# 51 zero products on TensorE instead of 64, in a kernel that chains a gated recurrence and a cosine-gated feed-forward layer

## The chip, the cores and the metric

The kernel runs on one core of a Trainium2 chip. The metric is the device time of one execution in microseconds (us), as the median of several executions. A core has a TensorE (PE) that multiplies matrices into PSUM, a VectorE (DVE), a ScalarE (ACT) and a GpSimd engine (POOL), each with its own queue of instructions that it works off in order, and a SyncE (SP) whose queue issues nearly all DMA transfers here. PSUM is used as eight banks of 128 x 512 float32. Engines wait for each other through semaphores.

## The reference

Inputs are q, k, v and f_logit of shape (4, 8, 768, 48) (batch, heads, sequence, head width), and two weight matrices w_in (384 x 2048) and w_out (2048 x 384).

```python
f = 1 / (1 + exp(-f_logit))
for t in range(768):
    state = f[:, :, t, :, None] * state + einsum('bhd,bhe->bhde', k[:, :, t], v[:, :, t])
    y[:, :, t] = einsum('bhd,bhde->bhe', q[:, :, t], state)
x = y.transpose(0, 2, 1, 3).reshape(3072, 384)
h = x @ w_in
out = (h * cos(h)) @ w_out
```

## The kernel before, in words

The sequence is cut into pieces of 256 tokens, three for each of the four batches: 12 pieces, called pairs (a pair holds two blocks of 128 tokens, g = 0 and g = 1). The recurrence inside a pair is done with matrix products. The feed-forward part works in 13 units, the first two of 128 tokens, the rest of 256.

The steps of a pair n, with the line of the instruction in the profile:

- `f`, `k`, `q`, `v`: loads (L298). `ex`, `ln`, `fx`, `fy` (L331 to L349): the gate and its logarithm on ACT. `ad` (L365): sums of two tokens' logarithms on POOL, into a tile `sp`.
- `cum` (L376, L382, PE): running sums of the logarithms into one bank. `eb` and `ei` (L397; L393 for the first two pairs, ACT): exponentials of these sums, tiles `b` and `bi`. They are the readers of that bank.
- `qa`, `ka`, `qm`, `km` (L340 to L353, L406): q and k times the gates, mostly on POOL, into the tile `qk`, in two halves .0 and .1. `vb`, `vt` (L199): v rounded to bfloat16 and rearranged. Each of these copies is placed on ACT or POOL.
- `tq`, `tk` (L437, PE): transposes of the two parts of a `qk` half into a bank; `qkt` (L199): the copy out of it, on DVE or ACT. Pairs 6 to 11 transpose by DMA instead.
- `sc` (L458, PE): scores into two banks; `am` (L463, DVE): the masked copy out of them.
- `ps` (L481, PE): what the pair adds to the state; `st` (L499) and `sz` (L505), both on DVE: the state carried on and decayed.
- `y` and `yi` (L533, PE): the output inside the blocks and from the state before, two banks; `xe` (L199, ACT or DVE): the copy out to `x`.

The steps of a unit m: `h` (L581, PE) multiplies x by a part of w_in into two banks, `co` (L586, ACT) takes the cosine, `g` (L563, DVE) multiplies both; `o` (L597, PE) multiplies by w_out, `ot` copies out and `out` stores. The weights arrive in float32 in buffers of the pool for `g` (`w0.i` for w_in, `w1.i` for w_out, L284) and are rounded by `wc0.i`, `wc1.i` (L199, POOL or ACT).

The order of the work is written out by hand in `ORDER`, a list of words such as `sc1.0:T2`: the step, the engine's letter (T for PE, V for DVE, S for ACT, G for POOL, Y for SP), and the buffers or PSUM banks that its results take. Each engine gets its steps in the order of this list, and semaphore waits follow from what the steps read and write. A step that writes a bank waits for the readers of what stood there before. Steps on different banks of one PSUM tile are declared independent by `apart`, which looks back over the last 12 users of the tile.

The zero products are the steps `zf0` to `zf63` (L266). Each is one product of a 128 x 128 and a 128 x 512 tile of zeros, started afresh and written into one PSUM bank that nothing reads. They stand among PE's steps from its first instruction up to `h1.01`. A zero product, too, waits until the bank that it writes has been read.

The part of PE's order around the change, from 16 to 34 us of the profile, is (numbers after T are banks; a step without one goes on in the bank that an earlier step of the same value opened): `tk1.1`, eight zero products (T0), `cum3:T0`, three zero products (T0), `tk1.0`, `yi0:T6`, `y0:T7`, three zero products (T2), `sc1.0:T2`, seven zero products (T4), `sc1.1:T0`, `cum2:T4`, `ps1.0:T6,7`, `ps1.1`, three zero products (T2), `h0.00:T2`, `h1.00:T4`, two zero products (T0), `h1.01`, `yi1:T6,0`, `y1`, `h0.01`, `h2.11:T0` and so on. The readers of `cum3`'s bank stand in ACT's order as `vb1`, `eb3`, `ei3`, `vt1.1`, `xe0.0`, `ei2`, `eb2`; DVE's order there is `qkt1.1`, `qkt1.0`, `sz0.11`, `xe0.1`, `am1.0`, `sz0.10`, `am1.1`, a clearing of a state tile, `st1.00`, `st1.01`, `sz1.01`, `sz1.00`, `st1.11`, `st1.10`, `xe1.0`.

Of the kernel before, what the change touches and what calls it, by code (L numbers as in the profile page):

```python
# [54 lines left out]
st1.01:V km2.1:G co1.0:S0 sz1.01:V0 sz1.00:V st1.11:V yi1:T6,0 y1:T h0.01:T st1.10:V xe1.0:V1  # L55
sz1.10:V0 sz1.11:V xe1.1:S co0.0:S1 h2.11:T0 h2.10:T g0.0:V2 g1.0:V1 co2.1:S2 g2.1:V3 w1.1:Y0
h2.01:T6 f4:Y2 w1.3:Y4 h2.00:T co2.0:S1 h2.20:T2 h2.21:T h1.10:T4 co2.2:S0 h1.11:T g2.0:V h2.31:T0
h2.30:T co1.1:S2 co2.3:S1 g2.2:V g1.1:V wc1.3:G tk3.1:T6 tq3.0:T7 tq3.1:T qkt3.1:S2 h0.11:T2 tk3.0:T
h0.10:T o3.2:T6 sc3.1:T4 v2:Y0 qkt3.0:S3 co0.1:S2 am3.1:V0 g0.1:V g2.3:V o3.0:T o2.0:T7 o1.2:T4
o2.2:T o1.0:T sc3.0:T2 o0.2:T5 tq2.0:T0 tq2.1:T1 o0.0:T tk2.0:T wc1.1:S ex4:S ln4:S1 v3:Y1 ad4:G2  # L60
fy4:S vb2:S1 tk2.1:T vt2.0:S1 fx4:S vt2.2:S vt2.1:S vb3:G0 vt3.0:S0 am3.0:V1 qkt2.0:V0 qkt2.1:V1
o2.1:T o3.1:T f5:Y0 ex5:S sc2.1:T0 am2.1:V2 sc2.0:T2 o0.1:T am2.0:V3 o1.3:T o2.3:T o3.3:T ot2:V0
ot3:V1 ps2.1:T2 ps2.0:T vt3.2:G st2.00:V st2.01:V sz2.01:V1 q4:Y1 cum4:T3 o0.3:T o1.1:T sz2.00:V
ot1:V2 ps3.1:T6,7 vt2.3:G ps3.0:T sz3.00:V2 sz3.01:V ln5:S1 y2:T2,0 yi2:T xe2.1:V0 vt3.3:G vt3.1:G
y3:T4,6 yi3:T xe3.0:V1 ad5:G2 xe2.0:S ei4:S0 fx5:S eb4:S0 h3.20:T0 cum5:T4 eb5:S1 ei5:S1 v5:Y2 v4:Y0
st3.11:V xe3.1:V ot0:V3 k4:Y0 h3.21:T co3.2:S1 sz3.11:V0 st3.10:V sz3.10:V qa4:G h4.10:T2 h3.11:T4
h3.10:T h4.11:T h3.01:T6 h3.00:T co3.1:S2 g3.2:V1 g3.1:V qm4.0:G1 qm4.1:G vb4:G0 vb5:G1 co4.1:S0
ka4:G co3.0:S1 k5:Y1 q5:Y0 km4.1:G ka5:G h4.20:T0 h4.21:T h3.31:T4 h3.30:T g4.1:V2 fy5:S co4.2:S2
co3.3:S0 g3.0:V g4.2:V km5.0:G2 km4.0:G qa5:G vt4.2:G0 vt4.3:G qm5.0:G h4.30:T2 f6:Y1 f7:Y2 h4.31:T
tk4.1:T6 tq4.1:T o5.2:T7 o4.2:T0 tq4.0:T1 co4.3:S1 vt4.0:S ex6:S v6:Y2 out1:Y q6:Y1 out3:Y k6:Y0  # L70
out0:Y q7:Y2 out2:Y v7:Y0 qm5.1:G km5.1:G vt4.1:G k7:Y1 qkt4.1:V2 g3.3:V g4.3:V tk4.0:T tk5.0:T6
o5.0:T o5.1:T qkt4.0:V3 ps4.0:T4,5 ps4.1:T sc4.1:T2 st4.01:V st4.00:V sz4.01:V2 ex7:S vt5.2:S1
ln7:S1 ln6:S0 sz4.00:V st4.11:V am4.1:V0 tq5.0:T o6.2:T1 st4.10:V o5.3:T ot5:S2 o6.3:T tq5.1:T4
tk5.1:T o4.3:T sc4.0:T2 ad7:G2 sz4.11:V1 sz4.10:V qkt5.0:S0 fy7:S fx6:S cum7:T6 vt5.0:G ad6:G0
o4.1:T o4.0:T vt5.1:G vt5.3:G ka6:G eb7:S0 ei7:S1 fy6:S cum6:T5 ot4:S3 eb6:S2 ei6:S0 km6.0:G1
km6.1:G sc5.0:T6 qkt5.1:V1 am4.0:V1 y4:T0,2 yi4:T sc5.1:T4 ps5.0:T3 ps5.1:T am5.0:V2 fx7:S xe4.0:S0
vb6:S0 xe4.1:S o6.1:T h4.01:T6 h4.00:T co4.0:S1 ps6.1:T2,0 ps6.0:T st5.00:V sz5.00:V0 am5.1:V0
st5.01:V sz5.01:V sz6.01:V2 sz6.00:V h5.00:T4 h5.01:T zvt.2:G g4.0:V h5.21:T2 h5.20:T qa6:G qm6.0:G
vt6.1:G2 zsz.3:G ka7:G co5.0:S0 vb7:S1 yi5:T6,7 y5:T o6.0:T vt7.3:G0 co5.2:S1 xe5.0:S1 ot6:S0
g5.0:V1 h5.30:T4 h5.31:T co5.3:S0 zsp.1:G vt7.2:G vt6.3:G qm6.1:G km7.1:G2 vt7.0:G vt6.0:G km7.0:G  # L80
qa7:G st6.11:V st6.10:V xe5.1:V h6.20:T6 f9:Y0 k9:Y2 f8:Y1 tq6.0:Y2 out5:Y tq6.1:Y0 sz6.10:V0
sz6.11:V h6.21:T g5.2:V co6.2:S1 vt6.2:S h5.10:T0 h5.11:T co5.1:S2 g5.3:V g6.2:V3 h6.10:T2 h6.11:T
co6.1:S1 ex9:S ln9:S0 ex8:S g5.1:V qm7.1:G qm7.0:G ad9:G1 v8:Y0 f10:Y2 tq7.1:Y1 out6:Y tq7.0:Y3
g6.1:V o9.2:T4 o8.2:T5 o9.0:T o9.3:T q8:Y2 v9:Y2 q9:Y1 ps7.0:T0,1 sc6.1:T2 ps7.1:T sc6.0:T6 st7.01:V
st7.00:V am6.1:V0 am6.0:V2 ln8:S1 vb8:G0 ad8:G0 zqk.0:G o8.1:T o8.0:T o9.1:T o7.0:T2 cum9:T3 o8.3:T
sz7.01:V1 sz7.00:V yi6:T0 st7.10:V y6:T6 cum8:T7 o7.2:T o7.1:T o7.3:T fx8:S st7.11:V sz7.10:V2
ot8:V0 ot9:V2 xe6.0:V0 ot7:V1 sz7.11:V ex10:S ln10:S1 xe6.1:S fx9:S eb8:S2 ei9:S1 h7.30:T4 ei8:S0
fx10:S v10:Y0 k8:Y1 eb9:S1 sc7.1:T6 sc7.0:T2 ad10:G1 ka9:G h7.31:T h6.30:T0 h6.31:T am7.1:V0
am7.0:V2 co7.3:S1 fy9:S fy8:S fy10:S co6.3:S2 km9.1:G2 vt8.3:G2 vt7.1:G qa8:G qa9:G yi7:T6,7 y7:T
qm8.0:G0 q10:Y0 h6.00:T2 h6.01:T co6.0:S0 vb9:S1 qm8.1:G ka8:G km8.1:G km9.0:G km8.0:G vt9.1:G0  # L90
g7.3:V2 qm9.1:G vt9.3:G qa10:G qm9.0:G xe7.0:V2 xe7.1:V g6.3:V h7.00:T4 h8.11:T6 h7.01:T co7.0:S2
vt8.1:S h7.10:T0 h8.10:T co8.1:S1 g6.0:V g7.0:V g8.1:V1 h7.11:T h7.20:T2 h7.21:T k10:Y0 f11:Y0
tq8.1:Y1 tq8.0:Y3 out8:Y co7.1:S0 h8.20:T4 h8.21:T tq9.0:Y0 g7.1:V o10.1:T6 o10.0:T o10.2:T o12.3:T7
cum10:T0 co8.2:S1 co7.2:S0 vt8.2:S out9:Y ei10:S0 vb10:S2 eb10:S0 ex11:S ln11:S1 vt10.0:G1 vt8.0:G
ad11:G1 ka10:G g8.2:V g7.2:V ps8.0:T4 ps9.0:T5,1 ps8.1:T ps9.1:T o10.3:T o12.0:T o12.2:T o12.1:T
h8.30:T2 st8.00:V sz9.00:V0 sz9.01:V st9.10:V st8.01:V sz8.00:V1 tq9.1:Y2 sz9.10:V3 st9.11:V
km10.1:G0 km10.0:G sz8.01:V sz9.11:V k11:Y1 h8.31:T sc8.1:T0 ot12:V0 co8.3:S0 ot10:S2 fy11:S vt9.0:G
qm10.0:G am8.1:V0 qm10.1:G q11:Y1 sc8.0:T4 am8.0:V2 o11.1:T7 o11.0:T o11.3:T yi8:T6,0 y8:T sc9.0:T4
g8.3:V cum11:T1 ei11:S0 eb11:S1 vt9.2:S fx11:S ka11:G km11.0:G2 km11.1:G qa11:G tq10.0:Y1 h8.01:T2
h8.00:T out4:Y xe8.0:S2 am9.0:V0 xe8.1:V v11:Y0 tq10.1:Y3 co8.0:S0 qm11.1:G vb11:G1 ps10.0:T4,5  # L100
ps10.1:T st10.01:V sc9.1:T0 am9.1:V2 o11.2:T o13.1:T6 o13.0:T h9.20:T0 h9.21:T tq11.1:Y4 vt11.1:G2
vt10.3:G qm11.0:G sz10.01:V1 st10.00:V sz10.00:V o13.2:T o14.2:T4 o13.3:T vt10.2:G vt11.2:G vt11.3:G
vt11.0:G co9.2:S1 g8.0:V st10.10:V st10.11:V vt10.1:S sz10.11:V2 sz10.10:V ot11:S3 sc10.0:T2 out7:Y
y9:T7,5 yi9:T g9.2:V3 o14.1:T h9.31:T0 h9.30:T xe9.0:S0 co9.3:S1 xe9.1:V am10.0:V0 tq11.0:Y0
sc10.1:T2 ps11.0:T5 ot13:S1 am10.1:V2 out10:Y out12:Y out11:Y out13:Y o14.0:T o14.3:T yi10:T2,3
y10:T xe10.0:S1 xe10.1:S sc11.1:T6 ps11.1:T g9.3:V ot14:S2 h9.00:T0 h9.01:T h11.21:T2 st11.01:V
am11.1:V0 st11.00:V sc11.0:T6 sz11.00:V1 sz11.01:V am11.0:V2 h11.20:T co9.0:S1 h11.31:T4 h11.30:T
g9.0:V yi11:T6,7 y11:T h10.11:T0 h10.10:T co11.2:S0 xe11.0:S3 co11.3:S1 xe11.1:V co10.1:S2 g11.2:V2
h12.01:T6 h12.00:T g11.3:V g10.1:V4 co12.0:S0 h10.20:T2 h10.21:T h12.20:T4 h12.21:T co10.2:S1
co12.2:S2 g12.0:V0 h9.11:T0 h9.10:T h10.01:T6 h10.00:T g10.2:V co9.1:S0 co10.0:S1 g12.2:V g9.1:V  # L110
g10.0:V h12.10:T2 h12.30:T4 h12.31:T co12.3:S0 g12.3:V h11.11:T0 h11.10:T co11.1:S1 h11.01:T6
h12.11:T h11.00:T g11.1:V co12.1:S0 co11.0:S2 o18.1:T4 g12.1:V g11.0:V o23.0:T5 o22.2:T0 o17.3:T1
o17.2:T h10.30:T2 h10.31:T o19.0:T6 o23.2:T co10.3:S2 o17.1:T o15.1:T7 o18.2:T o23.3:T g10.3:V
# [606 lines left out]
```

## Time and profile before

| | us |
|---|---|
| median of three runs | 193.93 (192.84 to 194.72) |
| the profiled execution, its whole time | 193.17 |
| its span, first to last instruction | 191.0 |
| PE busy in the span | 179.2 (94%) |
| DVE, ACT, POOL busy | 139.9, 133.8, 105.7 |
| zero products | 64, of which 60 have a record, 18.8 us busy |

The page of the profile gives busy time by engine, the span in 40 slices, the chain of work that ended last, and groups of instructions by line. The timeline gives, for a stretch, the start and the length of instructions in us, with the idle time before them and what ended it in brackets. Instructions of one line that follow each other are merged into one row with a count; the length then runs from the first's start to the last's end. The windows view gives busy time by engine for chosen stretches, the granted clock of TensorE as a share of full speed (PEclk), the share of the DMA engines and the rate.

### The profile page before, as it was taken

The page shows a single profiled execution, that of the slowest core. Times are in us where ns is not written, and L with a number is a line of the kernel's source. Part 1 is how long each engine was busy: PE and PEld are TensorE (multiplying, and loading weights), DVE is VectorE, ACT ScalarE, POOL GpSimd, SP SyncE. Part 2 cuts the span into 40 slices and gives each one's busy share as a digit, 9 for nine tenths or more (in the row PEclk, how much of TensorE's full clock was granted, in tenths as well). Part 3 has the DMA queues.
Part 4 walks back from the last instruction along what each step waited for, and adds up shares of the span by engine and source line. Part 5 has one row for each costly group of instructions (what it writes and reads, how often), then busy time and mean ns, then how long its engine had stood idle before and what let it go on. Part 6 is the DMA issues. An engine that isn't in the chain of part 4 may idle for free.

```text
span 191.0 us, 5843 instructions
## 1 busy us (share of the span) xinstructions
PE 179.2 (94%) x2470; PEld 127.6 (67%) x2474; DVE 139.9 (73%) x211; ACT 133.8 (70%) x190; POOL 105.7 (55%) x135
## 2 busy tenths in 40 slices
PE   7998299999996999999999999999999999999992
...
GB/s 155 262 261 319 364 323 352 137 321 291 199 262 156 16 307 317 252 20 160 90 228 228 263 228 97 123 210 155 161 121 193 3 3 0 0 3 0 124 117 171
DMA packets 70169, 33.40 MB, mean 175 GB/s; under 512 B 63232, under 2 KB 68608, under 8 KB 70144
## 3 DMA queue, kind: packets, MB, share of 16 engines
...
q10 hardware_dynamic: 672, 0.30, 0.5%
...
## 4 chain that ended last, share of the span: by engine, by line
PE 69%; DMA 9%; DVE 7%; ACT 6%; SPq 4%; issue 2%; POOL 1%; ACTq 0%; DVEq 0%
PE ps L597 28%; PE ps L581 27%; PE ps L533 5%; DVE g L563 5%; DMA v<-in_v_dram 4%; PE ps L458 3%; SPq L298 3%; DMA f<-in_f_logit_dram 3%; ACT co L586 3%; PE ps L266 2%; PE ps L437 2%; DMA k<-in_k_dram 1%; PE ps L481 1%; DVE ps L499 1%; DVE sz L505 1%
## 5 line engine op out<-in xcount | busy, mean ns | idle before, releaser
L563 DVE TENSOR_TENSOR g<-ps,co 128x1024 bf16<-128x1024 f32 x48 | 60.7, 1311 | 8.7 <-ACT co L586 7.5
L597 PE MATMUL ps<-w_out_bf,g 128*128 128x384 bf16 x384 | 67.0, 326 | 0.0
L581 PE MATMUL ps<-x,w_in_bf 128*128 128x256 bf16 (+1 forms) x624 | 66.8, 264 | 0.2
L586 ACT ACTIVATE co<-ps,halfpi 128x1024 bf16<-128x1024 f32 x48 | 52.6, 1114 | 14.6 <-PE ps L581 13.4
L581 PEld LDWEIGHTS <-w_in_bf 128*128 128x128 bf16 x624 | 56.6, 98 | 8.2 <-issue 0.3
L597 PEld LDWEIGHTS <-g 128*128 128x128 bf16 x384 | 36.1, 98 | 22.4
L463 DVE TENSOR_TENSOR am<-ps,pmask 128x1024 bf16<-128x1024 f32 x24 | 28.8, 1216 | 5.2 <-PE ps L458 4.7
L199 POOL COPY vt<-vb 64x384 bf16<-64x384 bf16 x34 | 16.8, 501 | 11.7 <-ACT vb L199 10.3
L266 PE MATMUL ps<-zero 128*128 128x512 bf16 x60 | 18.8, 439 | 4.8 <-ACT bi L397 3.1
L406 POOL TENSOR_TENSOR qk<-k,bi 128x384 bf16<-128x384 f32 x21 | 20.7, 1000 | 1.3 <-POOL k L353 0.7
L406 POOL TENSOR_TENSOR qk<-q,b 128x384 bf16<-128x384 f32 x20 | 19.8, 1000 | 2.9 <-ACT b L397 2.2
L199 ACT COPY ot<-ps 128x384 f32<-128x384 f32 (+1 forms) x13 | 5.9, 466 | 18.0 <-PE ps L597 16.9
L199 DVE COPY ot<-ps 128x384 f32<-128x384 f32 (+1 forms) x13 | 6.3, 507 | 15.1 <-PE ps L597 14.9
L365 POOL TENSOR_TENSOR sp<-ls 128x384 bf16<-128x384 f32 x10 | 10.0, 996 | 12.2 <-ACT ls L335 7.4
L505 DVE TENSOR_TENSOR sz<-ps,b 64x192 bf16<-64x192 f32 x40 | 13.9, 354 | 1.7 <-PE ps L481 0.8
L353 POOL TENSOR_TENSOR k<-k,f 128x384 f32<-128x384 f32 (+1 forms) x12 | 11.4, 950 | 4.2 <-DMA k<-in_k_dram 2.8
L266 PEld LDWEIGHTS <-zero 128*128 128x128 bf16 x64 | 6.2, 108 | 11.0 <-issue 6.4
L499 DVE TENSOR_TENSOR ps<-ps,sz 64x192 f32<-64x192 f32 x32 | 11.7, 366 | 2.4 <-PE ps L481 1.4
L331 ACT ACTIVATE f<-f 128x768 f32<-128x768 f32 (+1 forms) x14 | 10.3, 746 | 3.1 <-DMA f<-in_f_logit_dram 3.0
L199 ACT CAST x<-ps 128x384 bf16<-128x384 f32 x12 | 5.7, 484 | 8.8 <-PE ps L533 8.8
L343 POOL TENSOR_TENSOR q<-f,q 128x384 f32<-128x384 f32 x10 | 9.9, 999 | 2.3 <-issue 2.1
L199 DVE COPY qkt<-ps 128x1024 bf16<-128x1024 bf16 x9 | 6.1, 687 | 5.5 <-PE ps L437 5.4
...
## 6 DMA issues: line engine op xcount, KB each, us to landing
...
```

The lines of the kernel that those rows point to most:

```text
L199: (nc.scalar.copy if e == "ACT" else eng(e).tensor_copy)(out=o, in_=i)
L266: G.step(f"zf{i}", ("PE",), lambda e, dump=dump: nc.tensor.matmul(dump.ap, lhsT=zero[:, 0:128], rhs=zero, start=True, stop=True), writes=[ ...
L331: nc.scalar.activation(out=flat(t.ap), in_=flat(t.ap), func=AF.Exp, scale=-1.0)
L353: eng(e).tensor_mul(out=w.ap[:, :, 0, :], in0=w.ap[:, :, 0, :], in1=t.ap[:, :, 0, :])
L406: G.step(f"{nm}{n}.{u}", ("POOL", "DVE") if cut else ("POOL",), lambda e, u=u, j=j, src=src, dec=dec: eng(e).tensor_mul(out=qkp[u][j].ap[: ...
L463: G.step(f"am{n}.{u}", ("DVE",), lambda e, u=u, sc=sc: nc.vector.tensor_mul(out=am[u].ap.rearrange("p r b n -> p (r b) n"), in0=sc.ap.rear ...
L499: nc.vector.tensor_add(out=view()[s], in0=view()[s], in1=S0.ap[s, :, r, :])
L505: eng(e).tensor_mul(out=new.ap[s, :, r, :].rearrange("p (u a) n -> p u a n", u=2), in0=view()[s].rearrange("p (u a) n -> p u a n", u=2), i ...
L563: nc.vector.tensor_mul(out=o.rearrange("p b (n e) -> p b e n", e=2), in0=ph.ap.rearrange("p (b e n) -> p b e n", e=2, n=64), in1=co.ap.rea ...
L581: nc.tensor.matmul(ph.ap[:, i * T:(i + 1) * T].rearrange("p (g t) -> p g t", t=C), lhsT=w_in_bf[:, kk, f0:f0 + 128], rhs=xa[:, :, kk, :], ...
L586: G.step(f"co{m}.{j}", ("ACT",), lambda e, ph=ph, co=co: nc.scalar.activation(out=co.ap, in_=ph.ap, func=AF.Sin, bias=halfpi), reads=[ph], ...
L597: nc.tensor.matmul(po.ap[:, 0:DM], lhsT=gT.ap[:, j, i * C:(i + 1) * C], rhs=w_out_bf[:, j, :], start=(po.first and j == 4 * s), stop=(po.f ...
```

## The change

Thirteen of the 64 zero products are taken out, and the rest are numbered anew. Those that go stand in five places of PE's order: two of the eight ahead of `cum3`, all three between `cum3` and `tk1.0`, two of the three ahead of `sc1.0`, three of the seven ahead of `sc1.1`, and all three between `ps1.1` and `h0.00`. All other steps keep their order on every engine, their buffers and their banks. In the program's waits, four change. The wait for `ei3`'s read of bank 0, which the first zero product after `cum3` carried, is now carried by `sc1.1`, the next step that writes this bank. `y0` now names the two copies to `vt` that it reads, and `h0.00` the read of its bank by `am1.0`; those had been covered by waits of steps ahead of them.

```diff
-ZEROS = 64
+ZEROS = 51
...
-zf43:T0 zf44:T0 zf45:T0 cum3:T0 w0.3:Y3 eb3:S2 ei3:S1 wc0.2:G qa3:G qm3.0:G1 k3:Y1 wc0.3:G w1.2:Y0
-w1.0:Y4 q2:Y1 k2:Y0 zf46:T0 zf47:T0 zf48:T0 tk1.0:T zsz.2:V am0.1:V0 am0.0:V1 st0.11:V qkt1.1:V2
-qkt1.0:V3 ka3:G km3.0:G km3.1:G qm3.1:G wc1.2:G yi0:T6 y0:T7 wc1.0:G qa2:G zf49:T2 zf50:T2 zf51:T2
-sc1.0:T2 zf52:T4 zf53:T4 zf54:T4 zf55:T4 zf56:T4 zf57:T4 zf58:T4 sc1.1:T0 cum2:T4 vt1.1:S xe0.0:S0
-sz0.11:V1 xe0.1:V am1.0:V0 sz0.10:V am1.1:V1 zsz.0:V ei2:S0 eb2:S0 ps1.0:T6,7 ps1.1:T zf59:T2
-zf60:T2 zf61:T2 h0.00:T2 h1.00:T4 qm2.1:G2 qm2.0:G ka2:G km2.0:G zf62:T0 zf63:T0 h1.01:T st1.00:V
+zf43:T0 cum3:T0 w0.3:Y3 eb3:S2 ei3:S1 wc0.2:G qa3:G qm3.0:G1 k3:Y1 wc0.3:G w1.2:Y0 w1.0:Y4 q2:Y1
+k2:Y0 tk1.0:T zsz.2:V am0.1:V0 am0.0:V1 st0.11:V qkt1.1:V2 qkt1.0:V3 ka3:G km3.0:G km3.1:G qm3.1:G
+wc1.2:G yi0:T6 y0:T7 wc1.0:G qa2:G zf44:T2 sc1.0:T2 zf45:T4 zf46:T4 zf47:T4 zf48:T4 sc1.1:T0 cum2:T4
+vt1.1:S xe0.0:S0 sz0.11:V1 xe0.1:V am1.0:V0 sz0.10:V am1.1:V1 zsz.0:V ei2:S0 eb2:S0 ps1.0:T6,7
+ps1.1:T h0.00:T2 h1.00:T4 qm2.1:G2 qm2.0:G ka2:G km2.0:G zf49:T0 zf50:T0 h1.01:T st1.00:V st1.01:V
...
```

More of the change, by code (lines that the diff above doesn't have):

```diff
@@ L54 @@
-zf60:T2 zf61:T2 h0.00:T2 h1.00:T4 qm2.1:G2 qm2.0:G ka2:G km2.0:G zf62:T0 zf63:T0 h1.01:T st1.00:V
[L55 to L113, printed above, removed]
@@ new lines @@
+k2:Y0 tk1.0:T zsz.2:V am0.1:V0 am0.0:V1 st0.11:V qkt1.1:V2 qkt1.0:V3 ka3:G km3.0:G km3.1:G qm3.1:G
+wc1.2:G yi0:T6 y0:T7 wc1.0:G qa2:G zf44:T2 sc1.0:T2 zf45:T4 zf46:T4 zf47:T4 zf48:T4 sc1.1:T0 cum2:T4
+vt1.1:S xe0.0:S0 sz0.11:V1 xe0.1:V am1.0:V0 sz0.10:V am1.1:V1 zsz.0:V ei2:S0 eb2:S0 ps1.0:T6,7
+ps1.1:T h0.00:T2 h1.00:T4 qm2.1:G2 qm2.0:G ka2:G km2.0:G zf49:T0 zf50:T0 h1.01:T st1.00:V st1.01:V
+km2.1:G co1.0:S0 sz1.01:V0 sz1.00:V st1.11:V yi1:T6,0 y1:T h0.01:T st1.10:V xe1.0:V1 sz1.10:V0
+sz1.11:V xe1.1:S co0.0:S1 h2.11:T0 h2.10:T g0.0:V2 g1.0:V1 co2.1:S2 g2.1:V3 w1.1:Y0 h2.01:T6 f4:Y2
@@ new lines @@
+w1.3:Y4 h2.00:T co2.0:S1 h2.20:T2 h2.21:T h1.10:T4 co2.2:S0 h1.11:T g2.0:V h2.31:T0 h2.30:T co1.1:S2
+co2.3:S1 g2.2:V g1.1:V wc1.3:G tk3.1:T6 tq3.0:T7 tq3.1:T qkt3.1:S2 h0.11:T2 tk3.0:T h0.10:T o3.2:T6
+sc3.1:T4 v2:Y0 qkt3.0:S3 co0.1:S2 am3.1:V0 g0.1:V g2.3:V o3.0:T o2.0:T7 o1.2:T4 o2.2:T o1.0:T
+sc3.0:T2 o0.2:T5 tq2.0:T0 tq2.1:T1 o0.0:T tk2.0:T wc1.1:S ex4:S ln4:S1 v3:Y1 ad4:G2 fy4:S vb2:S1
+tk2.1:T vt2.0:S1 fx4:S vt2.2:S vt2.1:S vb3:G0 vt3.0:S0 am3.0:V1 qkt2.0:V0 qkt2.1:V1 o2.1:T o3.1:T
+f5:Y0 ex5:S sc2.1:T0 am2.1:V2 sc2.0:T2 o0.1:T am2.0:V3 o1.3:T o2.3:T o3.3:T ot2:V0 ot3:V1 ps2.1:T2
@@ new lines @@
+ps2.0:T vt3.2:G st2.00:V st2.01:V sz2.01:V1 q4:Y1 cum4:T3 o0.3:T o1.1:T sz2.00:V ot1:V2 ps3.1:T6,7
+vt2.3:G ps3.0:T sz3.00:V2 sz3.01:V ln5:S1 y2:T2,0 yi2:T xe2.1:V0 vt3.3:G vt3.1:G y3:T4,6 yi3:T
+xe3.0:V1 ad5:G2 xe2.0:S ei4:S0 fx5:S eb4:S0 h3.20:T0 cum5:T4 eb5:S1 ei5:S1 v5:Y2 v4:Y0 st3.11:V
+xe3.1:V ot0:V3 k4:Y0 h3.21:T co3.2:S1 sz3.11:V0 st3.10:V sz3.10:V qa4:G h4.10:T2 h3.11:T4 h3.10:T
+h4.11:T h3.01:T6 h3.00:T co3.1:S2 g3.2:V1 g3.1:V qm4.0:G1 qm4.1:G vb4:G0 vb5:G1 co4.1:S0 ka4:G
+co3.0:S1 k5:Y1 q5:Y0 km4.1:G ka5:G h4.20:T0 h4.21:T h3.31:T4 h3.30:T g4.1:V2 fy5:S co4.2:S2 co3.3:S0
```

54 lines of the change are left out of this document (49 added, 5 removed).

## The prediction

> **What bounds the kernel now.** I read the page first: the span, PE's busy time in slices, and the group of zero products with the idle time ahead of it.
>
> ```profile
> span 191.0 us, 5843 instructions
> PE   7998299999996999999999999999999999999992
> L266 PE MATMUL ps<-zero 128*128 128x512 bf16 x60 | 18.8, 439 | 4.8 <-ACT bi L397 3.1
> ```
>
> PE is busy in nearly every slice but the fifth (19.1 to 23.9 us), and the zero products themselves once waited 3.1 us for an exponential on ACT. The windows view shows how full PE is behind that place.
>
> ```profile
> 34.00:62.00 28.00, 26.39 (x401) 19.64 (x397) 22.50 (x31) 21.49 (x28) 18.18 (x20) 1.00 0.95 227
> 62.00:188.00 126.00, 124.52 (x1718) 92.18 (x1716) 96.51 (x127) 92.19 (x122) 67.40 (x85) 1.00 0.58 133
> ```
>
> From 34 to 188 us PE is idle for 1.61 + 1.48 = 3.1 us in all, and at full clock. So TensorE is the bound there, the order is fixed, and what PE reaches earlier at 34 us the rest can keep, unless another engine or a load can't come earlier by as much. The timeline of the idle place, engine by engine:
>
> ```profile
> 19.41 0.32 PE L376 MATMUL ps<-sp,incl 128*128 128x384 bf16 x1 [0.73 <-POOL sp L365]
> ...
> 22.91 1.25 PE L266 MATMUL ps<-zero 128*128 128x512 bf16 x3 [3.10 <-ACT bi L397]
> 23.95 0.63 PE L437 MATMUL ps<-ident,qk 128*128 128x128 bf16 x4
> ...
> 19.31 0.99 POOL L406 TENSOR_TENSOR qk<-k,bi 128x384 bf16<-128x384 f32 x1
> ...
> 21.25 0.83 ACT L199 CAST vb<-v 128x768 bf16<-128x768 f32 x1 [1.60 <-DMA v<-in_v_dram]
> 21.99 0.49 ACT L397 ACTIVATE b<-ps 128x392 f32<-128x392 f32 x1
> 22.38 0.48 ACT L397 ACTIVATE bi<-ps 128x384 f32<-128x384 f32 x1
> 22.88 0.51 ACT L199 COPY vt<-vb 64x384 bf16<-64x384 bf16 x1
> ```
>
> This is the heart of it. `cum3` (L376) ends at 22.91 - 3.10 = 19.81. The three zero products behind it write the same bank 0, so they wait until `ei3` has read it. ACT can't do that earlier, because `vb1` stands ahead in its order and waits for the load of v until 21.25. So PE stands until 22.91, and runs three products of zeros, before it comes to `tk1.0` at 23.95. `tk1.0` writes bank 1 and needs only `km1.0`, which POOL finished at 19.31 + 0.99 = 20.30.
>
> **The clock.** In stretches of 3.4 us:
>
> ```profile
> 16.30:19.70 3.40, 2.67 (x22) 1.31 (x19) 3.27 (x6) 3.25 (x6) 1.89 (x3) 1.00 1.13 333
> 19.70:23.10 3.40, 0.30 (x6) 0.14 (x3) 0.41 (x1) 1.83 (x4) 3.40 (x5) 1.00 1.05 382
> 23.10:26.50 3.40, 3.07 (x52) 2.01 (x52) 1.61 (x3) 0.77 (x2) 3.15 (x5) 0.50 1.13 332
> ```
>
> After the stretch with 0.30 us of work PE is granted half its clock for 3.4 us, which costs 3.4 x 0.5 = 1.7 us of matmul time; after the stretch with 2.67 us it was not, and it was full again after one with 3.07.
>
> The Trainium skill, "TensorE: Matmul & The Clock Gate", Part 1, says that the array falls to half clock after an idle window of about 3.4 us, that the windows run free of the kernel's start, and advises against gaps over some 3 us between bursts. The trace agrees in the length (3.4 us at 0.50). As a general rule it speaks against taking fillers out; here the filler made the gap, and by the rule the sum below stands, as the longest gap left would be 19.41 - 18.24 = 1.2 us (worked out below).
>
> **The change part by part.** The rows that the sum is made of:
>
> ```profile
> 24.62 0.69 DVE L199 COPY qkt<-ps 128x1024 bf16<-128x1024 bf16 x1 [4.52 <-PE ps L437]
> ...
> 25.93 0.56 DVE L199 CAST x<-ps 128x384 bf16<-128x384 f32 x1 [0.23 <-PE ps L533]
> 27.35 1.22 DVE L463 TENSOR_TENSOR am<-ps,pmask 128x1024 bf16<-128x1024 f32 x1 [0.86 <-PE ps L458]
> 28.49 0.34 DVE L505 TENSOR_TENSOR sz<-ps,b 64x192 bf16<-64x192 f32 x1
> 29.36 1.23 DVE L463 TENSOR_TENSOR am<-ps,pmask 128x1024 bf16<-128x1024 f32 x1 [0.54 <-PE ps L458]
> ...
> 31.63 0.72 DVE L505 TENSOR_TENSOR sz<-ps,b 64x192 bf16<-64x192 f32 x2
> ...
> 16.78 1.89 PE L266 MATMUL ps<-zero 128*128 128x512 bf16 x8
> ...
> 26.91 0.40 PE L458 MATMUL ps<-qkt 48*128 48x128 bf16 x8
> ...
> 29.53 0.44 PE L481 MATMUL ps<-vb,qk 64*64 64x48 bf16 x32
> ...
> 30.56 1.50 PE L581 MATMUL ps<-x,w_in_bf 128*128 128x128 bf16 x24
> ...
> 33.09 0.52 PE L533 MATMUL ps<-qkt,sz 128*32 128x128 bf16 x24
> 33.44 0.62 PE L533 MATMUL ps<-am,vt 128*32 128x128 bf16 x32
> ```
>
> *Two of eight ahead of `cum3`:* a zero product at full clock takes 1.89 / 8, some 0.22 after the pipeline's tail. The last six end near 16.78 + 1.89 - 0.43 = 18.24, and `cum3` waits for POOL's `sp` until 19.41 as before. Worth nothing.
>
> *The three behind `cum3`:* `tk1.0` starts at 20.35 instead of 23.95, at full clock, and ends at about 20.75. `qkt1.0` on DVE (0.69), idle for 4.52 us now, ends at 21.5, `sz0.11` (0.34, as the other `sz`) at 21.85. `yi0` and `y0` follow `tk1.0` on PE: 12 of the first kind at 0.35/24 and 32 of the second in 0.62, 0.8 us, to 21.55; their copy `xe0.1` on DVE (0.56) ends at 22.4.
>
> *Two of three ahead of `sc1.0`, three of seven ahead of `sc1.1`:* `sc1.0` (0.40) comes after `qkt1.0` and one zero product, 21.75 to 22.1; four zero products bring PE to about 23.0. `am1.0` (1.22) runs from 22.4 to 23.65 and `sz0.10` to 23.95. `sc1.1` takes over the wait for `ei3`: 22.38 + 0.48 = 22.86, so it runs from 23.0 to 23.4. Queued behind it are `cum2` and `ps1`, and these need ACT's later `xe0.0` anyway. `am1.1` starts behind `sz0.10`, at 23.95, and ends at 25.2.
>
> *The state:* from `am1.1`'s end (29.36 + 1.23 = 30.59) to `sz1.00`'s (31.63 + 0.72 = 32.35) DVE needs 1.76 today, so `sz1.00` ends at 26.95, and `yi1`, which reads it, starts at 27.0.
>
> *The three ahead of `h0.00`, and PE's own way to `yi1`:* `xe0.0` on ACT follows `vt1.1` (22.88 + 0.51 = 23.39) and ends near 23.9; `ps1` 0.44, to 24.3; `h0.00` and `h1.00`, together 1.34 without the tail, to 25.65; two zero products that stay, to 26.1; `h1.01` 0.67, to 26.8. PE is there 0.2 us before DVE, so these three zero products are worth nothing by themselves beside DVE's chain; with them PE would be 0.65 later, at 27.4.
>
> **The sum:** `yi1` moves from 33.09 to 27.0, 6.1 us. Of this roughly 3.1 is the wait, 1.0 the three products (23.95 - 22.91), 1.7 the half clock, and 0.3 other products on the path.
>
> **What must follow.** Some things can't come earlier, as they hang on POOL, which is idle next in the 1.02 us ahead of 44.79, or on loads that POOL's work releases:
>
> ```profile
> 33.94 1.00 POOL L406 TENSOR_TENSOR qk<-q,b 128x384 bf16<-128x384 f32 x1
> ...
> 41.80 1.96 POOL L406 TENSOR_TENSOR qk<-k,bi 128x384 bf16<-128x384 f32 x2
> 44.79 1.46 POOL L199 CAST w_out_bf<-g 128x1536 bf16<-128x1536 f32 x1 [1.02 <-DMA g<-in_moe_w_out_dram]
> ...
> 41.41 0.83 PE L437 MATMUL ps<-ident,qk 128*128 128x128 bf16 x12
> ...
> 50.41 0.61 PE L437 MATMUL ps<-ident,qk 128*128 128x128 bf16 x8
> ...
> 60.85 0.29 PE L533 MATMUL ps<-am,vt 128*32 128x128 bf16 x6 [1.59 <-issue]
> ...
> 41.75 2.77 SPq L298 DMA_DIRECT2D f<-in_f_logit_dram  x1
> DMA to landing us min/median/max: 8.8/8.8/8.8
> ...
> 53.68 0.84 ACT L331 ACTIVATE f<-f 128x768 f32<-128x768 f32 x1
> 54.55 0.84 ACT L335 ACTIVATE ls<-f 128x768 f32<-128x768 f32 x1
> 58.76 0.48 ACT L199 CAST x<-ps 128x384 bf16<-128x384 f32 x1 [3.36 <-PE ps L533]
> ```
>
> `qm3.1` ends at 34.94; `tq3.1`, in the group of 12 transposes from 41.41, moves from about 41.8 to 35.7: 0.7 us spare. `km2.1` ends at 43.76; `tk2.1`, second in the group at 50.41, moves to about 44.5: 0.7 spare. The load of `f5` lands at 41.75 + 8.8 = 50.55; `ex5` and `ln5` then occupy ACT to 52.3, and `xe2.0` behind them moves from 58.76 to 52.65: 0.4 spare, the thinnest. So the whole 6.1 us fits, though barely; without that cover `xe2.0` would hold PE back by as much as ACT is late. Behind 62 us the loads are released by steps that move along.
>
> The profiled execution takes 193.17 (span 191.0 and 2.17 around it): 193.17 - 6.1 = 187.1. The median of the three runs is 0.76 higher, so against the median it would be 187.8; I take the middle, **187.4**.
>
> **The rivals.** *ACT or POOL pins the pairs 4 and 5.* `ex5` can come only 53.68 - 50.55 = 3.1 us earlier. If ACT has no slack behind it (its queue is dense from 44 to 55 us and its 3.36 us wait at `xe2.0` is what I spend), PE keeps only these 3.1 us: 193.17 - 3.1 = 190.1. Against it stands that wait.
>
> *The half clock stays, for one stretch.* In an unlucky position of the 3.4 us stretches, 18.2 to 21.6, PE would work `cum3` 0.4, `tk1.0` 0.4 and `yi0`, `y0` 0.8: 1.6 of 3.4 us, between the 0.30 that lost the clock and the 2.67 that kept it. Price at most 1.7: 188.8. The skill's page (Part 1) has the windows running free, so that this would differ from execution to execution.
>
> *The half clock comes to stay, and the kernel gets slower.* If 1.6 of 3.4 us loses the clock and the sparser fill afterwards doesn't win it back, PE goes cold into the h products (dense and bound from 28 us on). Each such stretch costs 1.7 us; beyond 6.1 / 1.7 = 3.6 stretches (12 us at half clock) the change loses, and with five the time is 193.17 - 6.1 + 8.5 = 195.6. Against it: at half clock the same work fills the stretch twice as well, and 3.07 us of work brought the clock back today.
>
> *The wait only moves.* `tk1.0` might be held until about 22.9 by something that the wait for `ei3` hides now. Then only the products of zeros fall away, at most 1.04 and 0.3 us: 191.8 to 192. Against it: its one input ended at 20.30, and DVE, its reader, was idle.
>
> **How the numbers follow.** Forecast, 5 to 7.7 us gained (the upper end if the 1.59 us stall at 60.85, which waits for nothing shown, falls away too): 62%. Pinned near 190: 14%. One cold stretch, 188.8: 11%. The wait only moves: 7%. Slower by the clock: 6%. The range takes in all but the last two: 185.4 (193.17 - 7.7) to 191.0 (the pinned case, and the median's 0.76 over the profile). About 1% (1.9 us, the width of the three runs) is what a measurement tells from no change. Faster 0.87, same 0.07, slower 0.06.
>
> **What would show it.** Right: the wait of 3.1 us is gone, `tk1.0` starts near 20.4, the granted clock stays at 1.00 between 19 and 30 us, `sc1.1` is what waits for `bi`, `yi1` starts near 27, PE is as dense as before after 28 us, and the span is near 185. Wrong: a granted clock of 0.5 in the h products, or new idle time of PE between 34 and 62 us, put down to POOL `qk`, to ACT `x` or to loads.

## The result, and the profile after

The kernel with 51 zero products takes 188.37 us in the median (187.83 to 189.99, five runs), beside 193.46 for the kernel before in the same session: a ratio of 0.974, with a 95% interval of 0.968 to 0.979. The profiled execution took 188.07, with a span of 185.9. The forecast was 187.4, and 187.1 against the profile; so 1.0 us of the expected 6.1 is missing.

The page of the kernel after, with the span, PE's busy tenths in 40 slices, the granted clock, and the group of the zero products:

```profile
span 185.9 us, 5821 instructions
...
PE   7998796999989999999999999999999999999992
...
PEclk9999999999999999999999999999999999999999
...
L264 PE MATMUL ps<-zero 128*128 128x512 bf16 x51 | 15.3, 430 | 1.2 <-DVE zero L203 1.2
```

The hole in the fifth slice has gone, and the zero products wait for nothing but the tile of zeros itself, at the start. Lines in this kernel are two less than before (L264 for L266 and so on). PE's four longest waits after 19 us, as the view that sums them by what ended them has them (total, times, longest):

```profile
PE ps L579 <- issue: 1.6, 1, 1.6
PE ps L374 <- POOL sp L363: 1.1, 1, 1.1
PE ps L531 <- issue: 1.1, 1, 1.1
PE ps L435 <- POOL qk L404: 0.6, 1, 0.6
```

The wait of 3.1 us for `bi` isn't there. In its place the first row is new: 1.6 us in the products h (L579) that wait for nothing the profile shows. The timeline of PE around the change:

```profile
20.22 0.40 PE L435 MATMUL ps<-ident,qk 128*128 128x128 bf16 x4 [0.56 <-POOL qk L404]
...
22.90 0.40 PE L456 MATMUL ps<-qkt 48*128 48x128 bf16 x8
...
26.79 0.52 PE L531 MATMUL ps<-qkt,sz 128*32 128x128 bf16 x24
27.12 0.63 PE L531 MATMUL ps<-am,vt 128*32 128x128 bf16 x32
27.69 0.28 PE L579 MATMUL ps<-x,w_in_bf 128*128 128x128 bf16 x2
29.54 7.48 PE L579 MATMUL ps<-x,w_in_bf 128*128 128x128 bf16 x82 [1.56 <-issue]
...
55.92 0.27 PE L531 MATMUL ps<-qkt,sz 128*32 128x128 bf16 x5 [1.06 <-issue]
```

`tk1.0` starts at 20.22 and `yi1` at 26.79, 6.30 us earlier than before. Two products into `h0.01`, PE stops for 1.56 us. The old stall of 1.59 in `y3` is one of 1.06 in `yi3` now. So 6.30 - 1.56 + (1.59 - 1.06) = 5.3 us should be left at 62 us; the span is 191.0 - 185.9 = 5.1 shorter. The windows show the same, and the clock:

```profile
16.30:19.70 3.40, 2.25 (x18) 1.07 (x15) 3.27 (x6) 3.15 (x6) 2.04 (x3) 1.00 1.12 331
19.70:23.10 3.40, 2.88 (x69) 1.68 (x69) 2.67 (x5) 1.98 (x4) 3.40 (x5) 1.00 1.05 384
23.10:26.50 3.40, 3.25 (x81) 2.82 (x76) 3.29 (x8) 2.72 (x5) 3.15 (x5) 1.00 1.13 332
26.50:30.00 3.50, 1.93 (x73) 1.56 (x70) 2.14 (x6) 1.49 (x2) 3.42 (x4) 1.00 1.13 330
34.00:62.00 28.00, 26.80 (x399) 19.87 (x397) 21.84 (x32) 22.49 (x30) 22.60 (x25) 1.00 0.91 229
62.00:182.00 120.00, 119.23 (x1670) 87.94 (x1669) 93.61 (x122) 87.04 (x116) 62.92 (x80) 1.00 0.59 138
```

The columns are the stretch, its length, the busy time of PE, PEld, DVE, ACT and POOL, the granted clock, the DMA share and GB/s. The clock is 1.00 everywhere; PE loses 3.50 - 1.93 = 1.6 us between 26.5 and 30, a stretch in which it was busy throughout before (3.50 of 3.50); behind 34 us it is as dense as it was.

### The profile page after: what moved, and what is told of

Read it like the earlier page. It is cut to its first block, busy times and chain, and to the rows that moved or that the text cites. A ratio compares the mean times of both kernels' runs of the same rounds, so it can differ in the third digit from the quotient of the medians.

```text
span 185.9 us, 5821 instructions
## 1 busy us (share of the span) xinstructions
PE 175.5 (94%) x2461; PEld 125.8 (68%) x2461; DVE 139.8 (75%) x211; ACT 134.1 (72%) x190; POOL 105.8 (57%) x135
## 4 chain that ended last, share of the span: by engine, by line
PE 68%; DMA 9%; DVE 7%; ACT 7%; SPq 4%; issue 3%; POOL 1%; ACTq 0%; DVEq 0%
PE ps L595 29%; PE ps L579 27%; DVE g L561 5%; PE ps L531 4%; DMA v<-in_v_dram 4%; SPq L296 3%; DMA f<-in_f_logit_dram 3%; ACT co L584 3%; PE ps L456 3%; PE ps L435 2%; DMA k<-in_k_dram 2%; PE ps L479 1%; DVE ps L497 1%; DVE sz L503 1%; ACT vt L197 1%
## 5 line engine op out<-in xcount | busy, mean ns | idle before, releaser
L579 PE MATMUL ps<-x,w_in_bf 128*128 128x256 bf16 (+1 forms) x624 | 67.0, 264 | 1.7 <-issue 1.6
L579 PEld LDWEIGHTS <-w_in_bf 128*128 128x128 bf16 x624 | 56.5, 98 | 9.7 <-issue 2.2
L264 PE MATMUL ps<-zero 128*128 128x512 bf16 x51 | 15.3, 430 | 1.2 <-DVE zero L203 1.2
L456 PE MATMUL ps<-qkt 48*64 48x128 bf16 (+1 forms) x288 | 9.2, 220 | 0.8 <-ACT f L347 0.4
L264 PEld LDWEIGHTS <-zero 128*128 128x128 bf16 x51 | 5.0, 108 | 6.6 <-issue 2.8
L456 PEld LDWEIGHTS <-qkt 48*64 48x64 bf16 (+1 forms) x288 | 5.9, 102 | 4.8 <-issue 3.5
```

Of the source, the lines that this page charges most:

```text
L264: G.step(f"zf{i}", ("PE",), lambda e, dump=dump: nc.tensor.matmul(dump.ap, lhsT=zero[:, 0:128], rhs=zero, start=True, stop=True), writes=[ ...
L456: nc.tensor.matmul(o[t0:t1, r, 2 * a + g, :].rearrange("p (e n) -> p e n", e=2), lhsT=wide[s, t0 // 64, :] if turned else wide[s].rearrang ...
L579: nc.tensor.matmul(ph.ap[:, i * T:(i + 1) * T].rearrange("p (g t) -> p g t", t=C), lhsT=w_in_bf[:, kk, f0:f0 + 128], rhs=xa[:, :, kk, :], ...
```

## The experiments

**The theory after the result:** the 6.3 us at `yi1` are the forecast mechanism, and the missing 1.0 is the fetch of PE's own instructions. PE's 4,900 or so instructions arrive in 19 transfers of 16 KB on a queue of their own, some 256 instructions each:

```profile
q8 instruction: 19, 0.31, 0.7%
```

(The columns are packets, MB and share of the DMA engines.) Counted from the kernel's steps, 351 products stand ahead of the first stall and 382 between the two. Each product is two instructions, a load of its weights and the product itself, so the stalls are some 764 instructions apart, close to three blocks of 256, which are 768. (An expectation below counts a few other instructions of PE too, and has 707 and 1474.) **The rivals:** the stall belongs to `h0.01` (its bank, its weights); the gain comes from the smaller number of products and not from the three behind `cum3`; the gain is the clock.

### Only the three behind `cum3` taken out

```diff
-... k2:Y0 zf46:T0 zf47:T0 zf48:T0 tk1.0:T
+... k2:Y0 tk1.0:T
```

> The kernel before without the three zero products behind cum3 alone, 61 in all. Theory (the wait for the read of bank 0 and the half clock that follows are the gain): tk1.0 near 20.3, clock 1.00 from 19 to 30 us, yi1 near 28 (5 us earlier than before, as the other ten products still stand in TensorE's way), and a short stall of TensorE without a named wait around 28.5 us; 188.5 to 189. Rival (each zero product that goes is worth its own time): 3 of 13 products, so about a quarter of the gain, 192.2.

Measured: 188.09 (187.23 to 188.78, four runs), ratio 0.975 (0.966 to 0.984): as fast as the whole change. In the profiled execution (188.78) `tk1.0` starts at 20.54, but `yi1` only at 30.11, since the clock fell in the middle:

```profile
16.30:19.70 3.40, 2.42 (x16) 1.11 (x14) 3.27 (x6) 3.17 (x6) 1.72 (x3) 1.00 1.12 332
19.70:23.10 3.40, 2.84 (x64) 1.55 (x62) 1.95 (x4) 1.67 (x4) 3.40 (x5) 0.83 1.05 381
23.10:26.50 3.40, 3.40 (x24) 1.31 (x20) 1.59 (x3) 0.93 (x2) 3.15 (x6) 0.67 1.14 336
```

That is the one cold stretch of the prediction's second rival. There is no stall in `h0.01`, and only 0.20 in `y3`: a PE that comes later finds its instructions there. So three of the 13 products are enough for the result. What the other ten do isn't told by this.

### Only the other ten taken out

```diff
-... zf49:T2 zf50:T2 zf51:T2 sc1.0:T2 zf52:T4 ... zf58:T4 sc1.1:T0
+... zf47:T2 sc1.0:T2 zf48:T4 ... zf51:T4 sc1.1:T0
```

(and the two ahead of `cum3` and the three ahead of `h0.00`; `zf46` to `zf48` behind `cum3` stay, renumbered.)

> The other half: the three products behind cum3 stay, the other ten go, 54 in all. Theory: the 3.1 us wait and the half clock stay; VectorE's chain gains about 1 us at yi1, part of which a stall in the instruction stream may take back; 192.3 to 193.5. Rival (products are worth their own time): three quarters of the gain, 189.6.

Measured: 192.3 (190.9 to 193.4, ten runs), ratio 0.995 (0.990 to 1.000), as expected. The wait (3.09) and the half clock stay. `yi1` moves by 1.67 to 31.42, more than I had given these ten, but 0.68 comes back as a stall in `y1` that the profile puts down to nothing, and 1.52 stands in `yi3`:

```profile
33.06 0.23 PE L532 MATMUL ps<-am,vt 128*32 128x128 bf16 x1 [0.68 <-issue]
```

### The three in another bank

```diff
-zf46:T0 zf47:T0 zf48:T0
+zf46:T3 zf47:T3 zf48:T3
```

> All 64 products stay, in the same places; only the bank that the three behind cum3 write is another, bank 3 instead of bank 0. Theory: the wait and the half clock go as in the change; tk1.0 near 20.5, and the products that stay cost TensorE some 1.6 us more than the change up to yi1 (near 28.6, 4.5 us earlier than before); without a stall at 28 us the end is near that of the change, 188.7 to 189.5. Rival (the number of products): as before, 193.5.

Measured: 190.98 (189.8 to 192.3, ten runs), ratio 0.990 (0.984 to 0.996). The experiment missed its aim: bank 3 isn't free at that place. It holds half of the scores `sc0.1`, and the products clear it before `am0.1` has copied them out, so this kernel leaves a part of pair 0's scores out. `am0.1` now waits for the products and PE for `am0.1`:

```profile
20.32 0.40 PE L437 MATMUL ps<-ident,qk 128*128 128x128 bf16 x4
22.88 0.51 PE L533 MATMUL ps<-qkt,sz 128*32 128x128 bf16 x12 [2.16 <-DVE am L463]
```

It shows that `tk1.0` comes at 20.3 when nothing ahead of it waits for `ei3`, and that here too a filler in a bank that is still needed makes a hole, only later. It doesn't separate the number from the place; the next one does.

### All 64, the three ahead of `cum3`

```diff
-... zf45:T0 cum3:T0 ... k2:Y0 zf46:T0 zf47:T0 zf48:T0 tk1.0:T
+... zf45:T0 zf46:T0 zf47:T0 zf48:T0 cum3:T0 ... k2:Y0 tk1.0:T
```

> The kernel before with all 64 products; only the three behind cum3 stand ahead of it, in the same bank 0, so that none of them meets a pending reader. Theory of the place: tk1.0 starts near 20.3, the 3.1 us wait is gone, the ten other products cost at most 0.7 to 1 us on PE's path to yi1 (near 28), and the time is 188 to 190, depending on the clock and on whether the fetch of the next instructions stops PE in y1 for up to 1.6. Theory of the number (the products cost time because they are many): 64 products as before, so no more than 0.5 us gained, 193.3.

Measured: 188.14 (187.4 to 188.35, four runs), ratio 0.970 (0.965 to 0.974). No product less, and as fast as the change. The theory by number has fallen.

```profile
16.84 2.54 PE L266 MATMUL ps<-zero 128*128 128x512 bf16 x11
19.40 0.32 PE L376 MATMUL ps<-sp,incl 128*128 128x384 bf16 x1
...
20.36 0.40 PE L437 MATMUL ps<-ident,qk 128*128 128x128 bf16 x4 [0.56 <-POOL qk L406]
...
28.36 0.52 PE L533 MATMUL ps<-qkt,sz 128*32 128x128 bf16 x24
```

PE's windows from 16.3 to 30 are all at 1.00 here, so this kernel also prices the clock. From `tk1.0` to `yi1` PE does the same instructions as before: 28.36 - 20.36 = 8.00 us at full clock, 33.09 - 23.95 = 9.14 before. The half clock cost 1.1 us on this way. In the changed kernel the same way takes 26.79 - 20.22 = 6.57, so the products that are missing there are worth 1.4.

### The instruction stream moved, in the changed kernel

The first 19 zero products of the changed kernel are each cut into four of 128 columns. The zeros are the same, but PE has 114 instructions more in the first 10 us, so all later ones stand elsewhere in the blocks of 256.

```diff
+SPLIT = 19
...
-            G.step(f"zf{i}", ("PE",), lambda e, dump=dump: nc.tensor.matmul(
-                dump.ap, lhsT=zero[:, 0:128], rhs=zero, start=True, stop=True), writes=[dump])
+            def products(e, dump=dump, w=128 if i < SPLIT else 512):
+                for c in range(0, 512, w):
+                    nc.tensor.matmul(dump.ap[:, c:c + w], lhsT=zero[:, 0:128], rhs=zero[:, c:c + w], start=True, stop=True)
+            G.step(f"zf{i}", ("PE",), products, writes=[dump])
```

> The changed kernel with its first 19 zero products cut into four of 128 columns each: the same columns in the same time, but 57 more products, 114 more instructions ahead of all else. Theory (the stall of 1.56 us in the middle of h0.01, and that of 1.06 us in the middle of yi3, which no wait explains, are TensorE waiting for the next 256 instructions of its program; both stand before the matmul that is 707 and 1474 in its order, three times 256 apart): these places move by 114 instructions into stretches with longer matmuls, both stalls go, and the gain of 6.3 us at yi1 is kept: 185.5 to 186.5. Rival (a hidden wait of h0.01 for a load or a cast): the stall stays two matmuls into h0.01, at 188.4.

Measured: 185.21 (184.99 to 185.28, four runs), ratio 0.960 (0.952 to 0.968). Neither stall is left. PE runs through `h0.01` unbroken:

```profile
27.77 7.58 PE L582 MATMUL ps<-x,w_in_bf 128*128 128x128 bf16 x84
```

And these are all its waits of 0.2 us and more after 17 us:

```profile
PE ps L438 <- POOL qk L407: 0.6, 1, 0.6
PE ps L459 <- ACT f L350: 0.4, 1, 0.4
PE ps L377 <- POOL sp L366: 0.4, 1, 0.4
PE ps L459 <- DVE g L564: 0.2, 1, 0.2
PE ps L534 <- DVE sz L506: 0.2, 1, 0.2
```

Once more, on one chip beside the changed kernel, with five rounds for each:

> The changed kernel with the moved stream once more, beside the changed kernel on the same chip: 185.2, that is 3.0 to 3.2 below the changed kernel, if the two stalls (1.56 and 1.06, with what hangs on them) are the instruction stream's; a part of the runs 1 to 1.7 longer at a clock of 0.99 if the half clock comes by chance in this one too.

> The changed kernel once more, to see how often the half clock comes: one stretch of 3.4 us at half speed lowers the mean granted clock of the span to about 0.991. If the stretches run free of the kernel's start, a part of its runs shows 0.99 and is 1 to 1.7 longer than the rest near 188.2, as the one of 189.99 among the first five did; if that run was a thing of its own, all lie at 187.8 to 188.6 with a clock of 0.998 or more.

Measured: 185.39 (185.09 to 186.07, six runs, ratio 0.958, 0.956 to 0.961) for the moved stream, 188.33 (187.81 to 190.38, seven runs, ratio 0.973, 0.970 to 0.977) for the changed kernel: 2.9 us between the two. Of its seven runs, three show a mean clock of 0.988 to 0.990, at 190.38, 188.33 and 187.81. So half clock does come by chance, but two of these three are no longer than the rest. The profiled one is that of 190.38:

```profile
26.40:29.80 3.40, 1.71 (x68) 1.33 (x65) 2.37 (x7) 1.48 (x2) 3.32 (x4) 1.00 1.12 326
29.80:33.20 3.40, 3.39 (x22) 2.71 (x23) 0.98 (x1) 1.11 (x1) 3.32 (x4) 0.52 1.09 359
```

Here the stall itself (1.70 us, to 29.81) emptied a stretch of 3.4 us to 1.71 of work, and the next one ran at 0.52: 3.4 x 0.48 = 1.6 us lost in the dense products h. The clock's stretches can be found more exactly than by these cuts: in each of the seven traces where it fell within the kernel, it fell a whole number of 3.41 us after it had first risen to full (before: from 6.06 to 23.13, five times; here: from 6.05 to 29.94, seven times). Laid out so, this stretch of 1.71 lost the clock; in the profile after the same place, 26.05 to 29.47, held 1.91 and kept it, so that execution was close to losing it too. With the two stalls (1.70, 1.64) the sum is right: gain 6.16 at `yi1`, less 1.70 + 1.64 - 1.59, less 1.6, is 2.8; the span is 191.0 - 188.2 = 2.8 shorter.

### The stream moved in the kernel before

```diff
+SPLIT = 19
```

(and the same steps as in the moved stream, with all 64 products.)

> The kernel before with its 64 products, the first 19 of them cut into four products of 128 columns each (same zeros, 57 matmuls and 57 weight loads more, all in the first 10 us). It moves PE's later instructions by 114 places against the 16 KB blocks in which they are fetched, and leaves the wait behind cum3 alone. Theory of the instruction stream: the 1.59 us stall in y3 goes, about 1.5 us faster than before (ratio 0.992), the 3.1 us wait and the half clock stay. Rival, that the gain of the cut products in the changed kernel came from something else about the first 10 us (start, clock): then the stall at 60.85 stays. If the stall only moves to another product of the small ones, the ratio is 1.00.

Measured: 191.35 (189.99 to 193.01, ten runs), ratio 0.990 (0.984 to 0.996). The stall in `y3` has gone, the wait behind `cum3` stands (3.36), and half clock follows it (0.58 granted from 23.1 to 26.5, 0.92 from there to 30):

```profile
PE ps L269 <- ACT bi L400: 3.4, 1, 3.4
PE ps L461 <- ACT f L352: 0.4, 1, 0.4
PE ps L269 <- issue: 0.3, 1, 0.3
```

The span is 191.0 - 189.4 = 1.6 shorter, the length of that stall: the term is there without the change as well. The ten executions also price the clock: the three at 1.000 took 189.99 to 190.29, the four at 0.988 to 0.991 took 191.05 to 191.91.

### The border moved by three products

```diff
+SPLIT = 1
```

> The changed kernel with only its first zero product cut into four: three matmuls and three weight loads more at the very start, six instructions. If the 1.56 us stall stands at the border of a 16 KB block of PE's instructions, it moves by three products: from before the third product of h0.01 to before the last product of y1, and the one in yi3 moves three products earlier too; the time stays, 188.4 or so. If the stall belongs to h0.01 itself (its bank, its weights), it stays where it was.

Measured: 188.36 (one run). The stall moved to before the last of `y1`'s 32 products, exactly three earlier, and the other likewise (from the eighth product of `yi3` to its fifth). It is no matter of `h0.01`. The other traces agree: each zero product more or less moves both places by one product. The run with ten out, which has three zeros more than the changed kernel, stops before the same last product of `y1`. The later stall stands five products before the end of `yi3` with 51 zeros, eight with 54; and in `y3` ahead of it three before the end with 61, six with 64.

```profile
28.03 0.52 PE L534 MATMUL ps<-qkt,sz 128*32 128x128 bf16 x24
28.37 0.62 PE L534 MATMUL ps<-am,vt 128*32 128x128 bf16 x31
29.79 0.23 PE L534 MATMUL ps<-am,vt 128*32 128x128 bf16 x1 [0.80 <-issue]
```

A second thing is to be seen. This execution had a cold stretch (0.77 and 0.73 granted between 19.7 and 26.5), so `yi1` came at 28.03, 1.24 later than in the profile after. Yet PE went on at 29.79 in place of 29.54, because its stall was shorter by 0.76. The records of the instruction queue (its transfer that landed last before PE went on, in us) tell why:

```text
kernel                           16 KB landed   PE goes on
changed, profile after              28.04          29.54
changed, again (190.38)             28.11          29.81
changed, border three earlier       28.06          29.79
only the other ten out              31.60          33.06
```

PE goes on 1.5 to 1.7 us after the block has landed, and in these three executions with 51 zeros it landed at 28.0 to 28.1. What PE saves on its way to this place beyond that is handed back there. It is also why the change (188.3) is no faster than all 64 in another order (188.1): the change is at `yi1` 28.36 - 26.79 = 1.57 us earlier and then stands still for 1.56, while the other kernel, whose block had landed at 26.48, doesn't stop at this border.

### What the ten are worth when the stream doesn't stop PE

```diff
-... k2:Y0 zf46:T0 zf47:T0 zf48:T0 tk1.0:T
+... k2:Y0 tk1.0:T
...
+SPLIT = 19
```

> Without the three products behind cum3 (61 zeros), and with the first 19 cut into four as in the moved-stream run. Against that run it tells what the other ten products cost. If they stand on PE's path as worked out (0.65 us, three of them ahead of h0.00) and the clock stays full: 185.9 to 186.2. If a cold stretch of 3.4 us comes as in the run without the three products: 187.5. If they are worth nothing: 185.2.

Measured: 186.89 (186.86 to 187.31, four runs), ratio 0.965 (0.962 to 0.968), at full clock. The moved stream without the ten took 185.21 and 185.39, so they cost 1.5 to 1.7 us, more than the 0.65 expected. `yi1` starts at 28.09 against 26.63, 1.46 later. The profiled execution, at 187.31 the longest of the four, has a span that is longer by 2.1 (185.1 and 183.0); the rest of this stands at the very end, where ACT's last copy to `ot`, at 181.30 in place of 179.58, waits for a store of an earlier one.

### Six products more taken out

```diff
-... zf38:T0 zf39:T0 zf40:T0 zf41:T0 zf42:T0 zf43:T0 cum3:T0
+... cum3:T0
```

(of the moved stream; 45 zeros are left.)

> The changed kernel with the moved stream, and with the six products ahead of cum3 left out too (45 zeros): nothing is to be done by PE from 16.7 to 19.3 but wait for POOL's sp, and at least 2.3 of any 3.4 us that begin near 16.5 are idle. If some 1 us of work in a stretch of 3.4 us holds the clock, the time is that of the moved stream, 185.2, and these six products are worth nothing. If it doesn't, there is half clock for 3.4 us from about 20 on, yi1 comes up to 1.7 later, and the time is 186 to 187. The waits for sp and qk stay either way.

Measured: 186.0 (185.17 to 186.18, four runs), ratio 0.959 (0.955 to 0.962). The profiled execution (185.17) is as fast as the moved stream, and its clock stayed full as long as PE had work. PE works for 1.26 us between 16.3 and 19.7 there, but on the clock's own stretches, counted from where it first rose (4.46), no stretch is so empty: 2.21 from 14.70 to 18.11, and 1.84 from there to 21.53. So it doesn't show that a third of a stretch is enough. In the traces, such stretches of 0.31 to 1.71 us of work between 14 and 30 us lost the clock; around 1.9 it goes both ways (1.88 lost it in the run with three out, 1.84 here and 1.91 in the profile after kept it).

The other three executions were at 185.9 to 186.2, two of them with a clock of 0.990 and 0.991, but one with 0.997. In the profiled execution these six products bring nothing that PE needs. Whether they guard the clock in others, and what the 0.6 to 0.8 us of the median are, isn't settled by four runs.

### The sum over all kernels

The gain of the profiled executions should be the gain at `yi1` (33.09 less its start), less the two stalls, plus the 1.59 of before. For the changed kernel run again, the 1.6 of half clock behind `yi1` go off as well:

| kernel | `yi1` | stall in `y1` or `h0.01` | stall in `y3` or `yi3` | sum | span shorter by |
|---|---|---|---|---|---|
| changed | 26.79 | 1.56 | 1.06 | 5.3 | 5.1 |
| three out | 30.11 | 0 | 0.20 | 4.4 | 4.4 |
| ten out | 31.42 | 0.68 | 1.52 | 1.1 | 0.9 |
| all 64, three moved | 28.36 | 0 | 1.39 | 4.9 | 5.0 |
| before, stream moved | 33.18 | 0 | 0 | 1.5 | 1.6 |
| border three earlier | 28.03 | 0.80 | 0.82 | 5.0 | 4.9 |
| changed, stream moved | 26.63 | 0 | 0 | 8.1 | 8.0 |
| changed, stream moved, again | 26.72 | 0 | 0 | 8.0 | 8.1 |
| changed, again | 26.93 | 1.70 | 1.64 | 2.8 | 2.8 |
| the three in another bank | 31.93 | 0 | 0.25 | 2.5 | 2.5 |
| three out, stream moved | 28.09 | 0 | 0 | 6.6 | 5.9 |
| six more out, stream moved | 26.75 | 0 | 0 | 7.9 | 8.1 |

The one that is off by more than 0.2 is the execution with the late copies at its end.

## Why the prediction was right, and where it wasn't

*The wait and the three products:* right. `tk1.0` was forecast at 20.35 and came at 20.22, held by POOL's `qk` as worked out; 23.95 - 20.22 = 3.7 us of the gain stand here. That the wait would only move has fallen with it. One sign didn't come: `sc1.1`, which took over the wait for `ei3`, starts at 22.90 and doesn't have to wait, as `ei3` ends at 22.70 and the four zero products ahead of `sc1.1` last longer.

*The half clock:* right in kind, too large in size. The clock stayed full in the profile after. Behind `tk1.0` the half clock had cost 1.1 us (9.14 against 8.00), not 1.7. Another 0.4 lies ahead of `tk1.0`, as the three zero products took 1.04 before and 0.66 at full clock (23.04 to 23.70 in the kernel before with the stream moved); the sum has these 0.4 twice, in the 1.0 of the three products and in the 1.7. The page of the Trainium skill, "TensorE: Matmul & The Clock Gate", Part 1, has the windows free of the kernel's start; the executions bear that out, as four of the twelve of the changed kernel show a clock of 0.988 to 0.990 and eight one of 0.997 or more.

The kernel before changes with the clock too. Of its executions beside the experiments two ran at 0.998 and 0.999, and took 190.95 and 190.87; twelve fast ones at 0.988 to 0.991 took 192.28 to 193.57. So a good part of the distance between the medians (193.5 and 188.4) hangs on the clock, and more than these traces explain; no trace of an execution of the kernel before at full clock was kept, so this stays open.

*The ten others:* wrong. "With them PE would be 0.65 later" counted only the three ahead of `h0.00`, because I took DVE's chain to bind up to `yi1`. With all 64 in place PE has nearly no idle time from 20.36 to 28.36, so PE binds and the products between add up: 1.4 us in place of 0.3. The two wrong terms nearly cancel, which is luck: 3.7 + 1.1 + 1.4 is about the 6.3 at `yi1`, where 6.1 was forecast.

*What PE reaches earlier, the rest can keep:* this is the step that failed. I followed PE to `yi1` and took it as dense from there. The profile before shows no stall in `y1` or `h0.01`, for the wait behind `cum3` gave the fetch the time that it needed: in that trace the block landed at 29.33, when PE was still 122 products, some 245 instructions, short of the place. The new stall costs 1.56, the one in `yi3` gave back 0.53: 1.03 us, the size of the miss (188.07 against 187.07). The 0.2 by which `yi1` came earlier than forecast were lost elsewhere behind it. I had seen the 1.59 us stall, and let it only fall away, at the upper end of the gain; that the same cause could make a second one I didn't ask, since I took a stall without a shown cause for a thing of `y3`.

*What must follow:* right. With the moved stream the gain is larger than the forecast one, and the bounds are met. These are ACT's steps for pair 5 and `xe2.0` in that kernel:

```profile
50.28 0.84 ACT L332 ACTIVATE f<-f 128x768 f32<-128x768 f32 x1 [0.84 <-DMA f<-in_f_logit_dram]
51.16 0.85 ACT L336 ACTIVATE ls<-f 128x768 f32<-128x768 f32 x1
52.52 0.48 ACT L198 CAST x<-ps 128x384 bf16<-128x384 f32 x1 [0.51 <-PE ps L534]
```

`ex5` does wait for its load now (worked out 50.55, came 50.28), and `xe2.0` is at 52.52 (worked out 52.65) with 0.51 to spare (0.4). So ACT and POOL pin nothing behind `yi1`, neither here nor in the changed kernel, where `xe2.0` starts at 54.19 and ACT had been waiting for PE for 1.50.

*One cold stretch:* it does occur, in four of twelve executions of the changed kernel, oftener than 11% would have it. In the one trace where it lay ahead of the stalled fetch it cost 0.3 (188.36 with the border moved, against 188.07), and 1.6 in the one where it lay behind it. *Half clock to stay:* it didn't. No execution of the changed kernel had a mean clock below 0.988, and a single stretch makes 3.4 x 0.5 / 186 = 0.009. But half clock in the products h, which the prediction had named as a sign of being wrong, did come for one stretch in the execution of 190.38, by way of the new stall and not of the missing zeros.
